# Linear attention with a rational feed-forward: slots of 1024 columns in double-bank buffers, weights loaded in place, and a new plan of the order

## The chip, the cores and the metric

The kernel runs on one core of one Trainium2 chip. The metric is the device time in microseconds (us), from the start of the program to its end on that core; the time before is the median of three runs.

## The reference, cut to what matters

Inputs are r, k, v of shape 4 x 8 x 768 x 48 (batch, head, time, depth), w and u per head and depth, and the feed-forward's w_in (384 x 2048), w_out (2048 x 384), a (4 numbers) and b (2 numbers).

```python
for t in range(S):
    kt, vt, rt = (k[:, :, t], v[:, :, t], r[:, :, t])
    cur = np.einsum('bhd,bhe->bhde', u[None] * kt, vt)
    y[:, :, t] = np.einsum('bhd,bhde->bhe', rt, state + cur)
    state = w[None, :, :, None] * state + np.einsum('bhd,bhe->bhde', kt, vt)
...
h = x @ w_in
P = a[0] + a[1] * h + a[2] * h2 + a[3] * h3
Q = 1.0 + np.abs(b[0]) * np.abs(h) + np.abs(b[1]) * h2
g = P / (Q + 1e-06)
return (g @ w_out).astype(np.float32)
```

Here x is y with heads side by side (3072 x 384), and h2 and h3 are powers of h. The feed-forward weights come as 64-bit floats.

## The kernel before

The attention is cut into 24 blocks of 128 time steps (6 for each of 4 batches), handled with matrices inside a block and a carried state between blocks of a batch. A block loads r, k and v (L340), scales k and r by powers of w (L366, L370), forms the bonus of u (L374 to L388), transposes k and r on TensorE (`tk`, `tr`, L393), and makes the products `kv` (L438, L439), `a` (L416, L417) and `y` (L466). Then x is transposed (L485) into a high and a low part, `xthi` and `xtlo`.

The feed-forward has 12 tiles of 256 rows of x. A tile goes through 16 column blocks of 128 in w_in. A slot is two such blocks (`JG = 2`), so its h is 128 x 512, one PSUM bank; four banks rotate. The first product `f1` makes 9 matmuls of 256 columns for each block (L509: three pieces of the depth, each as high x high, high x low, low x high). Five steps on ScalarE (ACT) follow, `z` (absolute value, L540), `q` (square, L544), `t` (square, L549), `ln` (L554) and `ex` (L558), and five on VectorE (DVE), `u3` (L562), `hi` (L568), `p` (L572), `d` (L576) and `lo` (L580), which ends the slot's use of h. The second product `f2` makes three matmuls of 384 columns for each block and half tile (L513 to L515). The tile's output is copied by ACT (L613) and sent by SyncE (SP, L618).

The weights are split into a high and a low part in 28 pieces (12 of w_in, 16 of w_out). A piece is loaded into a staging tile that shares buffers with g (L253), changed on ACT and DVE, rounded on GpSimd (POOL, L278), and written as two parts into `wi_hi`, `wi_lo`, `wo_hi`, `wo_lo` (L281, L284).

The order of all this is not written out by hand. Each step is a task with a key, a planned duration, what it needs, and what buffers it takes. A planner (`run`) plays five engines through time: an engine that is idle takes the ready task with the smallest key whose buffers are free. The list that results is issued as it stands. Where TensorE finds no task and the planned time lies between the two numbers of `WARM` (L627: 1.6 and 132.098 us), the planner puts a dummy matmul there, 128 x 128 of ones into unused columns of an output bank (L898 to L905, issued at L914). A planned 0.0555 us stands for each. At the end every engine loads a flag (`okf`, L1006) and skips a general version of the kernel, which these inputs don't need.

Of the kernel before, what the change touches and what calls it, by code (L numbers as in the profile page):

```python
# [21 lines left out]
P = 128  # L22
HALF = 64
QC = float(np.float32(1.0) + np.float32(1e-6))
LN_SHIFT = 22
W_MIN, W_MAX = 0.5, 1.5
SIGN = -(1 << 31)
SMALL = 2.0 ** -40


@with_exitstack
def tile_linear_attention_rational_ffn(ctx, tc, r, k, v, w, u, w_in, w_out, a, b, out):
# [20 lines left out]
    ew = ctx.enter_context(tc.tile_pool(name="ew", bufs=3))  # L53
    ps_h = ctx.enter_context(tc.tile_pool(name="ps_h", bufs=4, space=PSUM))
# [17 lines left out]
    lnb = cst.tile([P, 3], F32, name="lnb")  # L72
# [23 lines left out]

    def pro_load():
        nc.sync.dma_start(wraw, w.rearrange("h d -> (h d)").rearrange("(c p) -> p c", p=P))
# [5 lines left out]
        nc.gpsimd.memset(wones, 1.0)  # L104
# [18 lines left out]
    def pro_beta():  # L123
        nc.scalar.activation(beta[:, 0:2], coef[:, 4:6], AF.Abs)
        nc.scalar.activation(cabs, coef, AF.Abs)

        nc.vector.tensor_scalar(rx, cabs[:, 3:6:2], SMALL, None, op0=ALU.max)
        nc.scalar.activation(half, rx, AF.Ln)
        nc.scalar.activation(root, half, AF.Exp, scale=0.5)
        nc.vector.memset(lnb[:, 0:1], QC * 2.0 ** -LN_SHIFT)  # L130
        nc.vector.memset(lnb[:, 1:2], -LN_SHIFT * math.log(2.0))


    def pro_squares():
# [5 lines left out]
        v_.reciprocal(half, root)  # L140
        v_.tensor_scalar(ctmp[:, 0:1], A3, 0.0, 0.5, op0=ALU.is_ge, op1=ALU.subtract)
# [98 lines left out]
    wi_hi = cst.tile([P, NCC, FF], F32R, name="wi_hi")  # L240
    wi_lo = cst.tile([P, NCC, FF], F32R, name="wi_lo")
    wo_hi = cst.tile([P, NJ, DM], F32R, name="wo_hi")
    wo_lo = cst.tile([P, NJ, DM], F32R, name="wo_lo")

    pieces = []

    def piece(hi, lo, src, n, nm):
        pieces.append({"hi": hi, "lo": lo, "src": src, "n": n, "nm": nm})

    def cv_load(c):  # L250
        n = c["n"]
        st = ew.tile([P, n, 2], I32, tag="g", name=f"st{c['nm']}")
        nc.sync.dma_start(st.rearrange("p n two -> p (n two)"), c["src"])  # L253
        c["top"], c["low"] = st[:, :, 1], st[:, :, 0]

    def cv_up(c):
        c["up"] = ew.tile([P, c["n"]], I32, tag="tc", name=f"up{c['nm']}", bufs=NTC)
        nc.scalar.activation(c["up"], c["low"].bitcast(U32), AF.Copy, scale=2.0 ** -29)

    def cv_exp(c, p):
        c["mag"] = pat("cp", p)[:, 0 : c["n"]]
        nc.scalar.activation(c["mag"], c["top"].bitcast(F32), AF.Copy, scale=2.0 ** -112)

    def cv_shift(c):
        m = c["mag"].bitcast(I32)
        nc.vector.tensor_scalar(m, m, 3, None, op0=ALU.logical_shift_left)

    def cv_sign(c):  # L270
        c["bits"] = ew.tile([P, c["n"]], I32, tag="tb", name=f"bits{c['nm']}")
        c["f"] = c["bits"].bitcast(F32)
        nc.vector.scalar_tensor_tensor(
            c["bits"], c["top"], SIGN, c["mag"].bitcast(I32), op0=ALU.bitwise_and, op1=ALU.bitwise_or
        )

    def cv_round(c):
        nc.gpsimd.tensor_tensor(c["bits"], c["bits"], c["up"], op=ALU.add)  # L278

    def cv_hi(c, e):  # L280
        copy(e, c["hi"], c["f"])  # L281

    def cv_lo(c, e):
        e.tensor_sub(c["lo"], c["f"], c["hi"].bitcast(F32))  # L284
# [218 lines left out]
    hps, gs, ops, oss = {}, {}, {}, {}  # L503

    def mm(o, j, hi, lo):
        n = 0
        for cc in range(NCC):
            for wt_, x_ in ((wi_hi, hi), (wi_hi, lo), (wi_lo, hi)):
                nc.tensor.matmul(o, wt_[:, cc, ts(j, P)], x_[:, cc], start=(n == 0), stop=(n == 3 * NCC - 1))  # L509
                n += 1  # L510

    def mm2(o, j, hi, lo):
        nc.tensor.matmul(o, hi, wo_hi[:, j], start=(j == 0), stop=False)  # L513
        nc.tensor.matmul(o, hi, wo_lo[:, j], start=False, stop=False)  # L514
        nc.tensor.matmul(o, lo, wo_hi[:, j], start=False, stop=(j == NJ - 1))  # L515


    SL = [(f, j, JG) for f in range(NTILE) for j in range(0, NJ, JG)]
    SL[-1:] = [(NTILE - 1, j, 1) for j in range(NJ - JG, NJ)]
    NS = len(SL)  # L520

# [24 lines left out]
    def ew_t(s):  # L546
        g = tiles(s)
        g["t"] = ew_tile(s, "tc", "t", bufs=NTC)
        nc.scalar.activation(g["t"], g["h"], AF.Square, scale=RA, bias=KA)  # L549

    def ew_ln(s):
        g = gs[s]
        g["z"] = ew_tile(s, "tb", "z")
        nc.scalar.activation(g["z"], g["q"], AF.Ln, scale=2.0 ** -LN_SHIFT, bias=lnb[:, 2:3])  # L554

    def ew_exp(s):
        g = gs[s]
        nc.scalar.activation(g["z"], g["z"], AF.Exp, scale=-1.0, bias=lnb[:, 1:2])  # L558
# [24 lines left out]
    def ew_general(s):  # L583
# [4 lines left out]
        t = ew_tile(s, "tc", "t", bufs=NTC)  # L588
# [3 lines left out]
        nc.scalar.activation(z, q, AF.Ln, scale=2.0 ** -LN_SHIFT, bias=lnb[:, 0:1])  # L592
        ew_exp(s)
# [8 lines left out]
    def f2(s, hf):  # L602
# [13 lines left out]
    def put_dma(f, hf):  # L616
# [4 lines left out]
    X0, DX0, DX1, DX2, DUE = 0.37, 7.61, 2.62, 3.94, 55.23  # L621
    AT = (
        -25.81, 17.05, -1.47, 56.83, 99.81, 143.46, 69.7, 148.52, 176.2, 128.58, 179.13, 132.24,
        194.38, 256.91, 197.64, 205.9, 149.09, 174.78, 262.97, 362.97, 354.01, 318.73, 358.59, 430.42,
    )
    CV0, DCV0, DCV1 = -48.38, 3.22, 1.32
    WARM = 1.6, 132.098  # L627
    HFREE = 1
    OFF = {
# [409 lines left out]
```

## Time and profile before

| what | value |
|---|---|
| median of 3 runs | 599.33 us (598.55 to 599.92) |
| profiled execution, first to last instruction | 597.1 us |
| TensorE busy | 579.9 us (97%) |
| VectorE busy | 518.9 us (87%) |
| ScalarE busy | 455.9 us (76%) |
| GpSimd busy | 178.3 us (30%) |
| matmuls in the profile | 6373, of which 896 are dummies |

All rows of the profile come from one execution; its span is 2.2 us under the median, and covers the first to the last instruction. PE is TensorE and PEld its loading of weights, which overlaps the matmuls. A matmul's duration contains its way through the array, so in a dense run the distance from start to start is the price of one, not the duration. A step of the idle column names what the engine waited for.

### The profile page before, as it was taken

Reading aid. Unit: us, or ns where it says so; the run is one execution under the profiler, and the core shown is the slowest. Engines: PE = TensorE matmul, PEld = TensorE weight load, DVE = VectorE, ACT = ScalarE, POOL = GpSimd, SP = SyncE. Lnnn points to the kernel's source line nnn. Section 1 sums busy time; section 2 is a strip of 40 time slices with the busy share of each in tenths; the row PEclk is TensorE's granted clock in tenths of the full one; section 3 lists DMA queues with packets and bytes.
Section 4 is the critical chain, followed back from the end, with each engine's and each line's share of the span. In section 5 each row is a group of like instructions: output and inputs, shape, how many; then the busy total and the mean of one; then the engine's idle time right before and its main releaser. Section 6 shows DMA issues by size and latency. Waiting matters only on the chain.

```text
span 597.1 us, 15392 instructions
## 1 busy us (share of the span) xinstructions
PE 579.9 (97%) x6373; PEld 560.5 (94%) x6373; DVE 518.9 (87%) x798; ACT 455.9 (76%) x765; POOL 178.3 (30%) x192
## 2 busy tenths in 40 slices
PE   8979999999999999999999998999999999999995
PEld 7968899999999999999999998999999999999995
DVE  5999999999989889889888799788899897878784
ACT  8728567887998987787687885888778767788883
POOL 6777887997541000003001076001240100000000
PEclk9979999999999999999999999999999999999998
DMA  9919365928050000002012132020220000000000
GB/s 194 194 41 216 96 147 131 237 85 167 14 94 1 27 1 23 6 2 60 1 26 63 28 75 54 0 53 22 43 57 4 14 29 2 1 27 1 27 2 32
DMA packets 92642, 34.31 MB, mean 57 GB/s; under 512 B 85906, under 2 KB 88980, under 8 KB 92564
## 3 DMA queue, kind: packets, MB, share of 16 engines
q1 hardware_dynamic: 92564, 33.24, 24.6%
q8 instruction: 52, 0.85, 0.6%
q14 instruction: 26, 0.21, 0.1%
HBM read 28.52 MB, written 4.72 MB: 56 GB/s over the span
## 4 chain that ended last, share of the span: by engine, by line
PE 78%; DVE 5%; POOL 2%; ACT 1%; DMA 1%; issue 1%; SPq 0%; DVEq 0%; POOLq 0%
PE h L509 32%; PE o L513 11%; PE o L515 10%; PE o L514 10%; PE o L914 3%; PE kv L438 3%; PE y L466 2%; PE a L416 2%; PE tk L393 1%; PE x L485 1%; PE tr L393 1%; DMA kh<-in_k_dram 1%; DVE ysa L427 1%; DVE vs L477 1%; DVE g L568 1%; DVE q L572 1%
## 5 line engine op out<-in xcount | busy, mean ns | idle before, releaser
L509 PE MATMUL h<-xthi,wi_hi 128*128 128x256 f32 x576 | 164.7, 286 | 0.0
L509 PE MATMUL h<-xthi,wi_lo 128*128 128x256 f32 x576 | 162.5, 282 | 0.0
L509 PE MATMUL h<-xtlo,wi_hi 128*128 128x256 f32 x576 | 162.5, 282 | 0.0
L513 PE MATMUL o<-wo_hi,g 128*128 128x384 f32 x384 | 132.2, 344 | 0.0
L515 PE MATMUL o<-wo_hi,g 128*128 128x384 f32 x384 | 129.0, 336 | 0.7 <-DVE g L580 0.7
L514 PE MATMUL o<-wo_lo,g 128*128 128x384 f32 x384 | 128.7, 335 | 0.0
L509 PEld LDWEIGHTS h<-xthi,wi_hi 128*128 128x128 f32 x576 | 109.4, 190 | 0.5
L509 PEld LDWEIGHTS h<-xthi,wi_lo 128*128 128x128 f32 x576 | 109.7, 190 | 0.0
L509 PEld LDWEIGHTS h<-xtlo,wi_hi 128*128 128x128 f32 x576 | 109.5, 190 | 0.0
L540 ACT ACTIVATE q<-h 128x512 f32<-128x512 f32 (+1 forms) x97 | 57.6, 594 | 67.3 <-PE h L509 63.3
L568 DVE SCALAR_TENSOR_TENSOR g<-h,sig,z 128x512 fp32r<-128x512 f32 (+1 forms) x97 | 72.1, 743 | 41.4 <-ACT z L558 37.3
L544 ACT ACTIVATE q<-q,off,root 128x512 f32<-128x512 f32 (+1 forms) x97 | 78.5, 809 | 0.4
L572 DVE SCALAR_TENSOR_TENSOR q<-q,sig,g 128x512 f32<-128x512 f32 (+1 forms) x97 | 75.3, 776 | 2.4
L549 ACT ACTIVATE t<-h,off,root 128x512 f32<-128x512 f32 (+1 forms) x97 | 74.7, 770 | 3.3 <-PE h L509 3.1
L562 DVE SCALAR_TENSOR_TENSOR h<-t,sig,h 128x512 f32<-128x512 f32 (+1 forms) x97 | 72.2, 744 | 4.7 <-ACT q L540 1.9
L576 DVE SCALAR_TENSOR_TENSOR h<-h,sig,q 128x512 f32<-128x512 f32 (+1 forms) x97 | 72.8, 751 | 2.6
L515 PEld LDWEIGHTS o<-wo_hi,g 128*128 128x128 f32 x384 | 72.1, 188 | 1.2 <-DVE g L580 1.2
L513 PEld LDWEIGHTS o<-wo_hi,g 128*128 128x128 f32 x384 | 72.4, 189 | 0.7
L514 PEld LDWEIGHTS o<-wo_lo,g 128*128 128x128 f32 x384 | 72.5, 189 | 0.0
L554 ACT ACTIVATE z<-q,lnb 128x512 f32<-128x512 f32 (+1 forms) x97 | 70.0, 722 | 2.4
L558 ACT ACTIVATE z<-z,lnb 128x512 f32<-128x512 f32 (+1 forms) x97 | 69.7, 719 | 2.5
L580 DVE TENSOR_TENSOR g<-h,z 128x512 fp32r<-128x512 f32 (+1 forms) x97 | 66.0, 680 | 1.3
(137 smaller groups left out, 988.8 us busy)
## 6 DMA issues: line engine op xcount, KB each, us to landing
sti<-in_moe_w_in_dram SPq DMA_DIRECT2D x12, 512.0 KB, 5.2
sto<-in_moe_w_out_dram SPq DMA_DIRECT2D x16, 384.0 KB, 3.2
vn<-in_v_dram SPq DMA_DIRECT2D x24, 192.0 KB, 3.4
rh<-in_r_dram SPq DMA_DIRECT2D x24, 192.0 KB, 3.7
kh<-in_k_dram SPq DMA_DIRECT2D x24, 192.0 KB, 4.6
out_dram<-os SPq DMA_DIRECT2D x24, 192.0 KB, 1.9
vs<-in_v_dram SPq DMA_DIRECT2D x18, 96.0 KB, 4.4
wraw<-in_w_dram SPq DMA_DIRECT2D x1, 1.5 KB
```

Source lines behind the costliest of these rows:

```text
L509: nc.tensor.matmul(o, wt_[:, cc, ts(j, P)], x_[:, cc], start=(n == 0), stop=(n == 3 * NCC - 1))
L513: nc.tensor.matmul(o, hi, wo_hi[:, j], start=(j == 0), stop=False)
L514: nc.tensor.matmul(o, hi, wo_lo[:, j], start=False, stop=False)
L515: nc.tensor.matmul(o, lo, wo_hi[:, j], start=False, stop=(j == NJ - 1))
L544: nc.scalar.activation(g["q"], g["q"], AF.Square, scale=RB, bias=KB)
L549: nc.scalar.activation(g["t"], g["h"], AF.Square, scale=RA, bias=KA)
L554: nc.scalar.activation(g["z"], g["q"], AF.Ln, scale=2.0 ** -LN_SHIFT, bias=lnb[:, 2:3])
L558: nc.scalar.activation(g["z"], g["z"], AF.Exp, scale=-1.0, bias=lnb[:, 1:2])
L562: nc.vector.scalar_tensor_tensor(g["h"], g["t"], KAP, g["h"], op0=ALU.add, op1=ALU.mult)
L568: nc.vector.scalar_tensor_tensor(g["hi"], g["h"], c0, g["z"], op0=ALU.add, op1=ALU.mult)
L572: nc.vector.scalar_tensor_tensor(g["q"], g["q"], qe, g["hi"].bitcast(F32), op0=ALU.add, op1=ALU.mult)
L576: nc.vector.scalar_tensor_tensor(g["h"], g["h"], c0, g["q"], op0=ALU.add, op1=ALU.subtract)
```

## The change

Feed-forward slots hold four column blocks (`JG = 4`), so h is 128 x 1024 and takes two PSUM banks; there are two such buffers, which the attention's products may also take one of. The last tile's slots are of 4, 4, 4, 2, 1 and 1 blocks. ACT's and DVE's ten steps of a slot are as before, but 1024 columns wide; `t` and `ln` write the same tile, so `ln` waits for `u3`, which reads `t`. The scale that `ln` and `ex` took as operands is folded into the constants of the prologue (`ROOT_SHIFT`, `SHIFT`).

Every weight piece has a tile of its own, into which it is loaded, in which it is changed, and in which its high and low part end; no staging tile is shared, and the loads wait for no buffer. Constants `coef` have early keys.

The planner moves out of the kernel's body (`graph`, `plan`), with one list of numbers K: a key for every tile, piece and block, and offsets for each kind of task, other ones for the first few of a kind. Dummies are added in groups of up to 64, up to the time of the next event; where no event is left, one at a time. `WARM` is now 1.6 and 1232.04.

```diff
+JG = 4
+SL = [(f, j, JG) for f in range(NTILE) for j in range(0, NJ, JG)]
+SL[-1:] = [(NTILE - 1, NJ - JG, 2), (NTILE - 1, NJ - 2, 1), (NTILE - 1, NJ - 1, 1)]
+CAP = {"g": 2, "tb": 2, "ta": 2, "cb": 3, "m": 6, "ldv": 3, "dt": 2, "os": 2, "xt": 2, "h": 2, "o": 1, "pa": 2}
...
+            add(("t", s), t + 5, {"A": 0.24 + 0.427 * x}, [("f1", s, nj - 1), ("sq",)], new=[("tb", ("z", s))], use=[h])
+            add(("ln", s), t + 8, {"A": 0.19 + 0.427 * x}, [("q", s), ("u3", s)], use=[("q", s), ("z", s)])
...
+    while events:
+        now = events[0][0]
...
+            if not done and e == "P" and w0 <= now < w1:
+                c = min(64, max(1, int((events[0][0] - now) / 0.0555) + 1)) if events else 1
+                order.append((("warm", c), e))
+                idle[e] = clock(now, 0.0555 * c, 128 * c)
+                seq += 1
+                heapq.heappush(events, (idle[e], seq, "engine", e))
...
+    'WARM': (
+        1.6, 1232.04,
+    ),
...
+    ps_h = ctx.enter_context(tc.tile_pool(name="ps_h", bufs=2, space=PSUM))
...
+    def cv_load(c):
+        st = cst.tile([P, c["n"], 2], I32, tag=c["tag"], name="s" + c["tag"])
+        nc.sync.dma_start(st.rearrange("p n two -> p (n two)"), c["src"])
+        c["top"], c["low"] = st[:, :, 1], st[:, :, 0]
...
+    def cv_hi(c):
+        c["w"] = whole[c["name"]] = cst.tile([P, 2, c["n"]], F32R, tag=c["tag"], name=c["tag"])
+        nc.scalar.copy(c["w"][:, HI], c["f"])
...
     def ew_ln(s):
         g = gs[s]
-        g["z"] = ew_tile(s, "tb", "z")
-        nc.scalar.activation(g["z"], g["q"], AF.Ln, scale=2.0 ** -LN_SHIFT, bias=lnb[:, 2:3])
+        nc.scalar.activation(g["z"], g["q"], AF.Ln, bias=QE)
...
-    WARM = 1.6, 132.098
...
+    def warm(count):
+        for _ in range(count):
+            o_ = ops[max(ops)][1] if ops else idle_bank
+            alone = not filling
+            nc.tensor.matmul(o_[:, DM:512], wones, wones, start=alone, stop=alone)
```

What the new numbers do to the order is shown at three places. The first is the end of TensorE's queue, where `o11_0` and `o11_1` are the two halves of the last tile's output and `okf` the flag. Before:

```order
L513 MATMUL o11_0_7855<-wo_hi_107,g96_8095 128x384
L514 MATMUL o11_0_7855<-wo_lo_108,g96_8095 128x384
L515 MATMUL o11_0_7855<-wo_hi_107,g96_8095 128x384
L513 MATMUL o11_1_7856<-wo_hi_107,g96_8095 128x384
L514 MATMUL o11_1_7856<-wo_lo_108,g96_8095 128x384
L515 MATMUL o11_1_7856<-wo_hi_107,g96_8095 128x384
L233 MATMUL fl0_8121<-identw_80,oks_103 1x128
L1006 TENSOR_LOAD okf_104
```

And now, where the pair of rows on `wones` is a dummy (weight load and matmul):

```order
L832 MATMUL o11_0_6962<-wo_15_1038,g49_7163 128x384
L833 MATMUL o11_0_6962<-wo_15_1038,g49_7163 128x384
L834 MATMUL o11_0_6962<-wo_15_1038,g49_7163 128x384
L832 MATMUL o11_1_6963<-wo_15_1038,g49_7163 128x384
L833 MATMUL o11_1_6963<-wo_15_1038,g49_7163 128x384
L834 MATMUL o11_1_6963<-wo_15_1038,g49_7163 128x384
L968 LDWEIGHTS wones_79
L968 MATMUL o11_1_6963<-wones_79 128x128
...
L1063 TENSOR_LOAD okf_104
```

Between the last product and the flag's load the pair on `wones` now stands 12,073 times; another 744 stand ahead of the last product, of which 229 open the queue. The flag's transpose has moved to an earlier place.

The second place is DVE's queue in the last quarter, where no attention is left beside the feed-forward (h, q, z and g with a slot's number are its tiles). Before, slots 82 and 83 of 512 columns:

```order
L562 SCALAR_TENSOR_TENSOR h82_7411<-t82_7449,sig_102,h82_7411 128x512
L568 SCALAR_TENSOR_TENSOR g82_7495<-h82_7411,sig_102,z82_7474 128x512
L572 SCALAR_TENSOR_TENSOR q82_7446<-q82_7446,sig_102,g82_7495 128x512
L562 SCALAR_TENSOR_TENSOR h83_7462<-t83_7499,sig_102,h83_7462 128x512
L576 SCALAR_TENSOR_TENSOR h82_7411<-h82_7411,sig_102,q82_7446 128x512
L580 TENSOR_TENSOR g82_7495<-h82_7411,z82_7474 128x512
L568 SCALAR_TENSOR_TENSOR g83_7534<-h83_7462,sig_102,z83_7521 128x512
```

And now, slots 42 and 43 of 1024 columns:

```order
L875 SCALAR_TENSOR_TENSOR h42_6614<-z42_6675,sig_102,h42_6614 128x1024
L881 SCALAR_TENSOR_TENSOR g42_6722<-h42_6614,sig_102,z42_6675 128x1024
L885 SCALAR_TENSOR_TENSOR q42_6672<-q42_6672,sig_102,g42_6722 128x1024
L889 SCALAR_TENSOR_TENSOR h42_6614<-h42_6614,sig_102,q42_6672 128x1024
L893 TENSOR_TENSOR g42_6722<-h42_6614,z42_6675 128x1024
L875 SCALAR_TENSOR_TENSOR h43_6693<-z43_6749,sig_102,h43_6693 128x1024
L881 SCALAR_TENSOR_TENSOR g43_6796<-h43_6693,sig_102,z43_6749 128x1024
```

The next slot's first step (`u3`, L562, now L875) stood between `p` and `d` of the slot at hand, and now stands behind its last step (`lo`, L893).

The third place is the head of SP's queue, which issues the loads (`sti`, `sto`, `swi`, `swo` are pieces of w_in and w_out, `wraw` is w). Before:

```order
L98 DMA wraw<-in_w_dram 128x3x1
L340 DMA vn_137<-in_v_dram 128x8x48
L340 DMA vn_147<-in_v_dram 128x8x48
L340 DMA rh_111<-in_r_dram 128x8x48
L340 DMA rh_113<-in_r_dram 128x8x48
L340 DMA kh_112<-in_k_dram 128x8x48
L340 DMA kh_114<-in_k_dram 128x8x48
L253 DMA sti_0_228<-in_moe_w_in_dram 128x1024
```

And now:

```order
L575 DMA swo_130<-in_moe_w_out_dram 128x768
L575 DMA swi_1_140<-in_moe_w_in_dram 128x1024
L575 DMA swi_0_161<-in_moe_w_in_dram 128x1024
L658 DMA vn_178<-in_v_dram 128x8x48
L658 DMA kh_108<-in_k_dram 128x8x48
L575 DMA swi_1_211<-in_moe_w_in_dram 128x1024
L575 DMA swo_243<-in_moe_w_out_dram 128x768
L658 DMA rh_107<-in_r_dram 128x8x48
L575 DMA swi_2_294<-in_moe_w_in_dram 128x1024
L441 DMA ur<-in_u_dram 1x384
L441 DMA wr<-in_w_dram 1x384
L575 DMA swo_357<-in_moe_w_out_dram 128x768
```

`wraw`, which stood first, comes next behind these twelve; weights stand ahead of r and k, and the last weight piece is the 52nd row of the queue.

More of the change, by code (lines that the diff above doesn't have):

```diff
@@ L71, in tile_linear_attention_rational_ffn @@
     beta = cst.tile([P, 2], F32, name="beta")
-    lnb = cst.tile([P, 3], F32, name="lnb")
+    lnb = cst.tile([P, 2], F32, name="lnb")
     A0, A1, A2, A3 = (coef[:, i : i + 1] for i in range(4))
@@ L237, in pro_flag_min, with wi_of @@
         nc.vector.tensor_copy(okf, oks[0:1, 1:2])
[L240 to L243, printed above, removed]
+    HI, LO = 0, 1
     pieces = []
-    def piece(hi, lo, src, n, nm):
-        pieces.append({"hi": hi, "lo": lo, "src": src, "n": n, "nm": nm})
+    whole = {}
+    def wi_of(j, cc, part):
+        return whole["i", j * P // CW, cc][:, part, ts(j % (CW // P), P)]
@@ L256, in cv_up @@
     def cv_up(c):
[L257 to L268, printed above, removed]
-    def cv_sign(c):
[L271 to L275, printed above, removed]
@@ L277, in cv_round, with cv_shift @@
-    def cv_round(c):
-        nc.gpsimd.tensor_tensor(c["bits"], c["bits"], c["up"], op=ALU.add)
-    def cv_hi(c, e):
-        copy(e, c["hi"], c["f"])
+        nc.scalar.activation(c["low"], c["low"].bitcast(U32), AF.Copy, scale=2.0 ** -29)
+    def cv_shift(c, p):
+        c["mag"] = pat("cp", p)[:, 0 : c["n"]].bitcast(I32)
+        nc.vector.tensor_scalar(c["mag"], c["top"], 3, None, op0=ALU.logical_shift_left)
+    def cv_sign(c):
+        nc.vector.scalar_tensor_tensor(c["top"], c["top"], SIGN, c["mag"], op0=ALU.bitwise_and, op1=ALU.bitwise_or)
@@ L507, in mm @@
         for cc in range(NCC):
-            for wt_, x_ in ((wi_hi, hi), (wi_hi, lo), (wi_lo, hi)):
-                nc.tensor.matmul(o, wt_[:, cc, ts(j, P)], x_[:, cc], start=(n == 0), stop=(n == 3 * NCC - 1))
+            for part, x_ in ((HI, hi), (HI, lo), (LO, hi)):
+                nc.tensor.matmul(o, wi_of(j, cc, part), x_[:, cc], start=(n == 0), stop=(n == 3 * NCC - 1))
                 n += 1
     def mm2(o, j, hi, lo):
[L513 to L520, printed above, removed]
+        nc.tensor.matmul(o, hi, wo_of(j, HI), start=(j == 0), stop=False)
+        nc.tensor.matmul(o, hi, wo_of(j, LO), start=False, stop=False)
+        nc.tensor.matmul(o, lo, wo_of(j, HI), start=False, stop=(j == NJ - 1))
     def f1(s, jj):
@@ L787, in tile_linear_attention_rational_ffn @@
-    COLS = {"turn": 256, "flagt": 256, "tk": 1024, "tr": 1024, "x": 768, "wp": 40, "ubp": 1536, "kv": 1180, "a": 1620, "y": 1736, "f1": 2304, "f2": 2304, "warm": 128}
-    TICK = 10.24 / 3
-    ticks = {}
-    def clock(t, dur, cols):
-        while dur > 1e-9:
-            k_ = int(t / TICK + 1e-9)
-            rate = 1.0 if ticks.get(k_ - 1, 0) >= 3060 else 0.5
-            step = min(dur / rate, (k_ + 1) * TICK - t)
-            ticks[k_] = ticks.get(k_, 0) + cols * step * rate / dur
-            cols -= cols * step * rate / dur
-            dur -= step * rate
-            t += step
-        return t
@@ L918, in tile_linear_attention_rational_ffn @@
+    def warm(count):
[3 more added lines that the diff above has]
+            nc.tensor.matmul(o_[:, DM:512], wones, wones, start=alone, stop=alone)
+    FN["warm"] = lambda e, count: warm(count)
+    order, banks, _, _ = plan(K)
+    bank.update(banks)
+    idle_bank = ps_o.tile([P, 512], F32, tag="o1", name="idle_bank")
     with tc.manual_schedule():
-        run()
+        for name, e in order:
+            FN[name[0]](ENG[e], *name[1:])
```

617 lines of the change are left out of this document (335 added, 282 removed), and 16 rows, old and new, of tables (K, OFF).

## The prediction, made before the changed kernel was run

> **What bounds the kernel now.** I read the page first: the engines' busy shares, and the chain of work that ended last.
>
> ```profile
> span 597.1 us, 15392 instructions
> PE 579.9 (97%) x6373; PEld 560.5 (94%) x6373; DVE 518.9 (87%) x798; ACT 455.9 (76%) x765; POOL 178.3 (30%) x192
> PE 78%; DVE 5%; POOL 2%; ACT 1%; DMA 1%; issue 1%; SPq 0%; DVEq 0%; POOLq 0%
> ```
>
> TensorE is busy for 97% of the span and is 78% of the chain. The kernel is a queue of matmuls, and its length is the time: 597.1 - 579.9 leaves 17.2 us without a matmul, some of it at both ends. Whatever is put into TensorE's queue therefore shows in the time at its full price, and whatever is saved on DVE or ACT shows only where TensorE waits for them. Next I read the busy time by stretches (columns: stretch, its length, PE, PEld, DVE, ACT, POOL with their counts, granted clock, DMA share, GB/s).
>
> ```profile
> 0.00:20.00 20.00, 17.38 (x298) 15.47 (x299) 12.85 (x23) 17.38 (x37) 13.81 (x30) 1.00 1.06 206
> 20.00:40.00 20.00, 16.56 (x274) 14.74 (x272) 19.17 (x30) 10.89 (x25) 15.72 (x15) 0.84 0.52 113
> 60.00:80.00 20.00, 19.31 (x350) 17.97 (x347) 19.75 (x28) 12.32 (x25) 17.05 (x16) 1.00 0.47 110
> 200.00:250.00 50.00, 50.00 (x354) 49.97 (x353) 44.36 (x63) 39.15 (x61) 0.00 (x0) 1.00 0.05 17
> ```
>
> Up to 140 us TensorE has gaps in its real work, and dummy matmuls fill them; from 200 us on the feed-forward keeps it full at clock 1.00. Third, the chain in such a full stretch, and the dummies in TensorE's timeline.
>
> ```profile
> 204.35 2.15 PE h L509 x18
> 208.59 2.15 PE h L509 x18
> 212.82 2.15 PE h L509 x18
> ...
> 2.08 3.17 PE L914 MATMUL warm<-wones 128*128 128x128 bf16 x28 [2.08 <-POOL wones L104]
> 5.04 0.63 PE L207 MATMUL ptab<-identw,pw 128*128 128x128 f32 x2
> ...
> 96.59 3.47 PE L914 MATMUL o<-wones 128*128 128x128 bf16 x59
> 99.87 0.42 PE L513 MATMUL o<-wo_hi,g 128*128 128x384 f32 x1
> ```
>
> A 512-column slot (18 matmuls of the first product, then 12 of the second) comes every (212.82 - 204.35) / 2 = 4.235 us. A dummy costs (99.87 - 96.59) us / 59 = 55.6 ns from start to start; the 28 at the very start cost (5.04 - 2.08) / 28 = 106 ns each. The groups by line give what all 896 dummies of the kernel before took:
>
> ```profile
> L914 PE MATMUL warm<-wones 128*128 128x128 bf16 x455 | 32.9, 235 | 2.1 <-POOL wones L104 2.1
> L914 PE MATMUL o<-wones 128*128 128x128 bf16 x441 | 27.3, 219 | 0.0
> ```
>
> That is 60.2 us, all before 141 us, as a planned time of 132.098 us ends them. The end of the program, from the timeline of all engines:
>
> ```profile
> 590.07 1.10 ACT L613 ACTIVATE os<-o,sig 128x384 f32<-128x384 f32 x2 [4.53 <-PE o L515]
> 590.22 0.34 PE L515 MATMUL o<-wo_hi,g 128*128 128x384 f32 x1
> ...
> 591.02 0.14 DVE L237 CAST okf<-oks 1x1 int32<-1x1 f32 x1
> ```
>
> The last product ends at 590.56. The last output and the flag follow at once, and 6.5 us of flag load, output landing and exit close the span.
>
> **The change, part by part.**
>
> *Dummies behind the last product.* The changed constant lets the planner add dummies until its own clock reads 1232.04 us, and it does so even when no task is left. The order shows the result: 744 dummies stand ahead of the last second product, and 12,073 behind it, in one block, ahead of TensorE's load of the flag. Nothing follows that could hide them: the outputs are written by ACT and SP meanwhile, and the program cannot end before TensorE has read the flag. The block costs 12,073 x 55.6 ns = 671.3 us. The bounds of the unit price are close: TensorE has no gap in the block, so the clock should stay at the 1.00 of the full stretch.
>
> *The real work on TensorE.* The same products in the same pieces are made, only grouped by four column blocks and not by two. With its first end at 590.56 and the 60.2 us of dummies taken out, 530.4 us are left. The 744 dummies inside cost about 30 x 106 ns while the clock is cold and 714 x 55.6 ns after, 3.2 + 39.7 = 42.9 us. The last product would end at 573.3 us, if TensorE waited as little as before.
>
> *Longer slots on ACT and DVE.* The groups with shapes kept apart, for the seven steps that follow each other from slot to slot in the new order:
>
> ```profile
> L572 DVE SCALAR_TENSOR_TENSOR q<-q,sig,g 128x512 f32<-128x512 f32 x95 | 74.3, 782 | 2.4
> L576 DVE SCALAR_TENSOR_TENSOR h<-h,sig,q 128x512 f32<-128x512 f32 x95 | 71.8, 756 | 2.5
> L562 DVE SCALAR_TENSOR_TENSOR h<-t,sig,h 128x512 f32<-128x512 f32 x95 | 71.2, 749 | 4.7 <-ACT q L540 1.9 <-ACT t L549 1.4
> L568 DVE SCALAR_TENSOR_TENSOR g<-h,sig,z 128x512 fp32r<-128x512 f32 x95 | 71.1, 748 | 41.4 <-ACT z L558 37.3 <-PE o L515 3.1 <-issue 0.2
> L554 ACT ACTIVATE z<-q,lnb 128x512 f32<-128x512 f32 x95 | 69.0, 726 | 2.4
> L558 ACT ACTIVATE z<-z,lnb 128x512 f32<-128x512 f32 x95 | 68.7, 723 | 2.5
> L580 DVE TENSOR_TENSOR g<-h,z 128x512 fp32r<-128x512 f32 x95 | 65.2, 686 | 1.2
> L554 ACT ACTIVATE z<-q,lnb 128x256 f32<-128x256 f32 x2 | 1.0, 508 | 0.0
> L558 ACT ACTIVATE z<-z,lnb 128x256 f32<-128x256 f32 x2 | 1.0, 508 | 0.0
> L576 DVE SCALAR_TENSOR_TENSOR h<-h,sig,q 128x256 f32<-128x256 f32 x2 | 1.0, 493 | 0.1
> L562 DVE SCALAR_TENSOR_TENSOR h<-t,sig,h 128x256 f32<-128x256 f32 x2 | 1.0, 487 | 0.0
> L572 DVE SCALAR_TENSOR_TENSOR q<-q,sig,g 128x256 f32<-128x256 f32 x2 | 1.0, 478 | 0.0
> L568 DVE SCALAR_TENSOR_TENSOR g<-h,sig,z 128x256 fp32r<-128x256 f32 x2 | 1.0, 476 | 0.0
> L580 DVE TENSOR_TENSOR g<-h,z 128x256 fp32r<-128x256 f32 x2 | 0.8, 420 | 0.0
> ```
>
> At 512 columns they sum to 5.17 us, at 256 to 3.37; every 256 columns add 1.80, so 1024 columns take 5.17 + 3.60 = 8.77 us, less than twice 5.17. Per slot DVE and ACT thus get cheaper. But where the feed-forward runs alone, DVE's new queue holds the first step of slot s+1 (u3) behind the last of slot s (lo), and ln now writes the tile that u3 has to read first: u3, ln, ex, hi, p, d, lo form a loop with no second slot in it. Two such steps in DVE's timeline show what lies between them:
>
> ```profile
> 577.31 0.75 DVE L568 SCALAR_TENSOR_TENSOR g<-h,sig,z 128x512 fp32r<-128x512 f32 x1 [0.65 <-ACT z L558]
> 578.10 0.75 DVE L572 SCALAR_TENSOR_TENSOR q<-q,sig,g 128x512 f32<-128x512 f32 x1
> ```
>
> That is 578.10 - 577.31 - 0.75 = 0.04 us. With six of these, some 0.2 us, the loop turns in 9.0 us, against 2 x 4.235 = 8.47 on TensorE. With only two double banks TensorE cannot run ahead of it. Some 27 slots stand in such stretches; 27 x 0.5 = 13.5 us is the most, and every stretch begins with a slot or so of slack. I take 8 us, and 0 and 14 as its ends. The copy of the second output half, between ln and ex in one slot of four, is in this margin. The steps that the change takes off DVE and ACT are worth nothing while TensorE bounds.
>
> *Loads and the start.* SP's queue now begins with weights, and w itself (wraw), on which the scaling of the first r and k rests, stands thirteenth, behind 3.9 MB; at the 206 GB/s of the first stretch that is 19 us. The 229 dummies that open TensorE's queue take 14.4 us of that, so little is added. All weight pieces go into places of their own and wait for no staging buffer; the last one has 16.4 MB ahead of it, itself included, which takes 80 us at 206 GB/s and 145 us at the 113 GB/s of the second stretch. The second product of slot 3, its first user, stands behind some 100 us of TensorE work. So there is no wait by the first rate, and 50 us with conversion by the second. The first rate is the nearer one, since DMA was saturated there (share 1.06) and at half load in the other (0.52). I take +4 us, with -10 (the 10.7 us of gaps ahead of the end going) and +45 as ends. The cheaper constants (two fewer scale operands, one multiplication more in the prologue) cost nothing that TensorE waits for.
>
> *Sum.* 573.3 + 8 + 4 = 585 us for the last product, 671 for the block, and 6 for flag and exit give a span of 1262.6; with the 2.2 us by which the median of 599.33 lies above the profiled span of 597.1, that is 1265 us. The measurement can tell about 0.2% from no change; this is 111% slower.
>
> **A rule against the unit price.** The row above spaces dummies by 55.6 ns over a run of 59. The Trainium skill's page "TensorE: Matmul & The Clock Gate", section "Back-to-back issue gap", says that a sustained stream of weight loads and matmuls in pairs is spaced by some 81 ns at 128 columns. By its figure the block would last 978 us and the kernel about 1572 us. The trace speaks against it, at 55.6 ns with a weight load ahead of every dummy; no run so far holds an unbroken block of this length, so it stays as a rival.
>
> **The rivals.**
>
> (a) The work part is late as well, and the last product ends above 630 us: weights at the slow rate, or attention steps put into the new loop. For it are the waits of the kernel before (engine, what it waited for: us in total, times, longest):
>
> ```profile
> POOL rh L370 <- DMA rh<-in_r_dram: 87.6, 7, 25.3
> POOL kh L366 <- DMA kh<-in_k_dram: 72.1, 6, 30.7
> ```
>
> POOL stood up to 30.7 us for one load, and DVE at 87% is the second bound. Against it: by the first stretch's rate the last weights are some 20 us ahead of their use. It gives 630 + 671 + 8 = 1309 us and more.
>
> (b) The long block runs at a wider spacing than 59 dummies show, as the clock falls or instructions come too slowly. At the cold row's 106 ns it would last 1280 us, and the kernel 1873 us. Against it: the full stretches keep clock 1.00 for 50 us and more, and from 60 to 80 us 697 instructions went through in 20 us, 28.7 ns each, where the block needs 27.8. The page's 81 ns would fall under this rival.
>
> (c) Faster: the block does not count. If time were taken up to the last output's landing, or if matmuls whose product nobody reads were not run, the price of the block would be zero and the kernel would come to 585 + 8 = 593 us or, without the loop and start terms, 581 us. It decides from 12,073 x 55.6 ns falling under 6 us. For it: no output depends on the block. Against it: the 60.2 us of dummies before were run as any matmul, and the median is above the span up to the last instruction, so time covers every engine's end.
>
> (d) The work part ends ahead of 560 us, and the kernel below 1240: the gaps and the hand-overs of the first 140 us nearly vanish.
>
> **How the numbers follow.** The forecast, 1240 to 1310 us, has 0.82: its low end is 585 less 8, 4 and the 10.7 us of gaps, with 671 and 8 added, its high end the bound of the loads (585 + 45). Rival (a) has 0.08, (b) 0.06, (c) 0.02, (d) 0.02. No more than 0.2 is left out by the forecast's own range, so the range is not widened. Faster by over 0.2% is (c) alone, 0.02; nothing leads to no change; slower is 0.98.
>
> **What would show it.** In the changed kernel's profile: TensorE's dummies as the costliest group, near 12,800 of them; DVE, ACT and POOL idle in the last half of the 40 slices, with TensorE at 9 there and PEclk at 9; the last second product between 560 and 630 us; DVE's u3 to u3 at 9 us in slots 14 to 21 and 41 to 46, and TensorE waiting there for lo. The forecast is wrong if the spacing in the block is not 55 to 57 ns, if the last product ends outside 560 to 630 us, or if the span ends well ahead of the block.

## The result and the profile after

| what | before | after |
|---|---|---|
| median of the runs | 599.3 us (598.55 to 599.92, 4 runs) | 1257.99 us (1257.75 to 1259.32, 4 runs) |
| ratio to before, with its interval | | 2.099 (2.096 to 2.102) |
| profiled execution, own time and span | | 1259.32 us, 1257.6 us |

The kernel takes 2.1 times as long, 7 us less than forecast. One execution of all behind this document, of the kernel before without its dummies, took 882.86 us at a granted clock of 0.56, for a reason that no run here shows; it is left out, and the median given for that kernel further down is of its other three. First the head of the page of after: span, busy time of the engines, some rows of the 40 slices (each 31.4 us here), and the shares of the chain that ended last.

```profile
span 1257.6 us, 38579 instructions
PE 1243.1 (99%) x18294; PEld 1221.6 (97%) x18294; DVE 468.6 (37%) x570; ACT 384.6 (31%) x508; POOL 171.5 (14%) x195
PE   8999999999999999999999999999999999999998
DVE  6898898787887877772000000000000000000000
ACT  7895685666656656661000000000000000000000
PEclk9899999999999999999999999999999999999999
PE 87%; DVE 3%; ACT 2%; issue 1%; POOL 0%; ACTq 0%; POOLq 0%
```

DVE and ACT fall silent in the 19th slice, near 580 us. TensorE goes on at a full clock for 21 more slices, alone. A page that showed only TensorE's 99% would read like a well-filled kernel. Which instructions fill it is shown by the groups by line, the costliest one of matmuls being

```profile
L968 PE MATMUL o<-wones 128*128 128x128 bf16 x12169 | 681.1, 219 | 0.7 <-ACT os L930 0.7
```

These are dummies, for 681.1 us. TensorE's timeline places them (start, duration, line, operation, and in brackets the idle time ahead of it and what ended it): the last second product, the first two rows of the block and its last one.

```profile
578.42 0.33 PE L834 MATMUL o<-wo,g 128*128 128x384 f32 x1
578.60 0.40 PE L968 MATMUL o<-wones 128*128 128x128 bf16 x4
579.66 10.54 PE L968 MATMUL o<-wones 128*128 128x128 bf16 x186 [0.67 <-ACT os L930]
...
1247.81 5.86 PE L968 MATMUL o<-wones 128*128 128x128 bf16 x102
```

The work ends at 578.6 us, the block at 1247.81 + 5.86 = 1253.7 us, and the program at 1257.6 us: 578.6 + 675.1 + 3.9. After four dummies the block stops for 0.67 us, for ACT, which still reads the bank into which they write; from then on it has no gap. Of its 12,073 dummies 12,069 stand behind that wait, (1253.67 - 579.66) us / 12,069 = 55.8 ns each. In the windows (columns as before), 100 us from the middle of the block and 50 us of the feed-forward alone:

```profile
600.00:700.00 100.00, 100.00 (x1795) 100.00 (x1793) 0.00 (x0) 0.00 (x0) 0.00 (x0) 1.00 0.01 2
500.00:550.00 50.00, 49.84 (x377) 49.16 (x377) 37.65 (x34) 32.98 (x34) 0.00 (x0) 1.00 0.03 12
```

100 us / 1795 = 55.7 ns, with a weight load beside each, at clock 1.00; a window also counts the few matmuls that reach into it from outside, so this agrees with 55.8. In the feed-forward DVE is at 75% and ACT at 66% of the stretch; before, from 200 to 250 us, they were at 89% and 78%.

### The profile page after: what moved, and what is told of

Read it like the earlier page. It is cut to its first block, busy times and chain, and to the rows that moved or that the text cites. A ratio compares the mean times of both kernels' runs of the same rounds, so it can differ in the third digit from the quotient of the medians.

```text
span 1257.6 us, 38579 instructions
## 1 busy us (share of the span) xinstructions
PE 1243.1 (99%) x18294; PEld 1221.6 (97%) x18294; DVE 468.6 (37%) x570; ACT 384.6 (31%) x508; POOL 171.5 (14%) x195
## 3 DMA queue, kind: packets, MB, share of 16 engines
q8 instruction: 145, 2.38, 0.8%
## 4 chain that ended last, share of the span: by engine, by line
PE 87%; DVE 3%; ACT 2%; issue 1%; POOL 0%; ACTq 0%; POOLq 0%
PE o L968 54%; PE h L828 13%; PE o L832 4%; PE o L834 4%; PE o L833 4%; PE y L784 2%; PE a L734 2%; PE kv L756 1%; PE tr L711 1%; PE tk L711 1%; PE x L803 1%; DVE g L881 1%; DVE h L875 1%; DVE q L885 1%; ACT z L867 1%
## 5 line engine op out<-in xcount | busy, mean ns | idle before, releaser
L968 PEld LDWEIGHTS <-wones 128*128 128x128 bf16 x12817 | 720.5, 98 | 4.8 <-POOL wones L424 2.1
L968 PE MATMUL o<-wones 128*128 128x128 bf16 x12169 | 681.1, 219 | 0.7 <-ACT os L930 0.7
L828 PE MATMUL h<-xthi,wi 128*128 128x256 f32 x1152 | 219.0, 284 | 1.0 <-DVE g L893 0.8
L828 PEld LDWEIGHTS h<-xthi,wi 128*128 128x128 f32 x1152 | 180.9, 188 | 3.0 <-issue 0.8
L828 PE MATMUL h<-xtlo,wi 128*128 128x256 f32 x576 | 160.8, 279 | 0.0
L832 PE MATMUL o<-wo,g 128*128 128x384 f32 x384 | 131.6, 343 | 0.0
L834 PE MATMUL o<-wo,g 128*128 128x384 f32 x384 | 129.2, 336 | 0.0
L833 PE MATMUL o<-wo,g 128*128 128x384 f32 x384 | 129.1, 336 | 0.0
L828 PEld LDWEIGHTS h<-xtlo,wi 128*128 128x128 f32 x576 | 108.4, 188 | 0.0
L832 PEld LDWEIGHTS o<-wo,g 128*128 128x128 f32 x384 | 72.2, 188 | 0.3
L833 PEld LDWEIGHTS o<-wo,g 128*128 128x128 f32 x384 | 72.3, 188 | 0.0
L834 PEld LDWEIGHTS o<-wo,g 128*128 128x128 f32 x384 | 72.2, 188 | 0.0
L875 DVE SCALAR_TENSOR_TENSOR h<-z,sig,h 128x1024 f32<-128x1024 f32 (+2 forms) x50 | 62.0, 1240 | 6.6 <-ACT z L863 6.4
L885 DVE SCALAR_TENSOR_TENSOR q<-q,sig,g 128x1024 f32<-128x1024 f32 (+2 forms) x50 | 63.4, 1269 | 1.3
L889 DVE SCALAR_TENSOR_TENSOR h<-h,sig,q 128x1024 f32<-128x1024 f32 (+2 forms) x50 | 62.3, 1246 | 1.3
L893 DVE TENSOR_TENSOR g<-h,z 128x1024 fp32r<-128x1024 f32 (+2 forms) x50 | 58.9, 1178 | 1.2
```

The costliest lines, as they stand in the source:

```text
L828: nc.tensor.matmul(o, wi_of(j, cc, part), x_[:, cc], start=(n == 0), stop=(n == 3 * NCC - 1))
L832: nc.tensor.matmul(o, hi, wo_of(j, HI), start=(j == 0), stop=False)
L833: nc.tensor.matmul(o, hi, wo_of(j, LO), start=False, stop=False)
L834: nc.tensor.matmul(o, lo, wo_of(j, HI), start=False, stop=(j == NJ - 1))
L875: nc.vector.scalar_tensor_tensor(g["h"], g["t"], KAP, g["h"], op0=ALU.add, op1=ALU.mult)
L885: nc.vector.scalar_tensor_tensor(g["q"], g["q"], qe, g["hi"].bitcast(F32), op0=ALU.add, op1=ALU.mult)
```

## The experiments

### Is it the block, and what does one dummy cost?

Theory: the block is paid in full, dummy by dummy, and has nothing to do with the new slots. Rival: a part of the 672 us belongs to the longer slots or the late loads. Three kernels tell them apart. The first leaves out every dummy behind the last product:

```diff
+    last = max(i for i, (n, e) in enumerate(order) if e == "P" and n[0] != "warm")
+    left = 0
+    kept = order[: last + 1]
+    for n, e in order[last + 1 :]:
+        if n[0] == "warm":
+            n = ("warm", min(left, n[1]))
+            left -= n[1]
+        if n[0] != "warm" or n[1]:
+            kept.append((n, e))
+    order = kept
```

> The changed kernel without the 12,073 dummies behind the last second product; all other instructions in the same order. Theory (every dummy of the block is paid in full): the last product stays at 579 us and the exit of 6 us as in the kernel before follows, so 585 to 587 us, 2.2% below the kernel before. Rival (the block covers something else that is slow in the new order, such as output copies or the flag): clearly more, above 592 us. Second rival (the loss lies in the longer slots, the block only fills it): near 1250 us.

Measured: 586.17 us, ratio to before 0.978 (0.974 to 0.981), span 584.9 us. The second keeps half of the block (`left = 6036`):

> The changed kernel with 6,036 dummies behind the last second product in the place of 12,073. Theory: the price is linear, 6,037 x 55.9 ns = 337.5 us less, so 920 to 921 us. Rival (a long run is spaced wider than a short one, from some length on): less than half of the block's 675 us goes with the first half of it, so a time away from 920 us by more than 5 us.

Measured: 919.95 us, ratio 1.536 (1.530 to 1.542). The third is the kernel before, with the block behind its order loop:

```diff
+        o_ = ops[max(ops)][1]
+        for _ in range(12073):
+            nc.tensor.matmul(o_[:, DM:512], wones, wones, start=True, stop=True)
```

> The kernel before, with 12,073 dummies put behind its last product, nothing else changed. Theory (the price belongs to the dummies and not to the new slots or plan): 599.3 + 675 less the 2 to 4 us of exit that now hide, so 1270 to 1275 us. Rival (the new slots and plan have a part in the loss): 1270 us is missed by more than 10 us.

Measured: 1271.21 us, ratio 2.123 (2.114 to 2.132). A window in the block of each, the half block's kernel first, then before with the block:

```profile
700.00:800.00 100.00, 100.00 (x1795) 100.00 (x1792) 0.00 (x0) 0.00 (x0) 0.00 (x0) 1.00 0.01 2
```

```profile
700.00:800.00 100.00, 100.00 (x1795) 100.00 (x1793) 0.00 (x0) 0.00 (x0) 0.00 (x0) 1.00 0.01 2
```

What follows: the block adds 1257.99 - 586.17 = 671.8 us to the changed kernel and 1271.21 - 599.01 = 672.2 us to the kernel before (599.01 us being its median beside these runs), 55.6 to 55.7 ns for each dummy. The first half of it adds 333.8 us and the second 338.0; the first is less because it hides the end of the last output. So the price is linear and the same in both kernels. The rival falls, and without the block the change is faster than before by 2.2% (1.9 to 2.6%).

### What does the loop through DVE cost?

The prediction put 8 us on the loop u3, ln, ex, hi, p, d, lo. DVE's timeline of after has it, u3 of three slots that follow each other and the wait for ex inside one of them:

```profile
522.79 1.28 DVE L875 SCALAR_TENSOR_TENSOR h<-z,sig,h 128x1024 f32<-128x1024 f32 x1
526.44 1.28 DVE L881 SCALAR_TENSOR_TENSOR g<-h,sig,z 128x1024 fp32r<-128x1024 f32 x1 [2.37 <-ACT z L871]
531.55 1.28 DVE L875 SCALAR_TENSOR_TENSOR h<-z,sig,h 128x1024 f32<-128x1024 f32 x1
540.32 1.28 DVE L875 SCALAR_TENSOR_TENSOR h<-z,sig,h 128x1024 f32<-128x1024 f32 x1
```

It turns in (540.32 - 522.79) / 2 = 8.77 us. TensorE, in the same stretch, begins first products at

```profile
523.80 0.28 PE L828 MATMUL h<-xthi,wi 128*128 128x256 f32 x1
...
532.17 0.28 PE L828 MATMUL h<-xthi,wi 128*128 128x256 f32 x1
...
540.54 0.36 PE L828 MATMUL h<-xthi,wi 128*128 128x256 f32 x1
...
549.31 0.35 PE L828 MATMUL h<-xthi,wi 128*128 128x256 f32 x1 [0.15 <-DVE g L893]
```

that is every 8.37 us, until the slack is used up and the last of these slots takes 8.77 us too. So the loop exists and is slower than TensorE by 0.4 us a slot. To break it, one kernel (without the block) puts u3 of slot s+1 ahead of lo of slot s in DVE's queue, wherever they are neighbours:

```diff
+    for s in range(1, NS):
+        at_ = {n: i for i, (n, e) in enumerate(order)}
+        dve = [n for n, e in order if e == "D"]
+        lo_, u3_ = ("lo", s - 1), ("u3", s)
+        if dve.index(u3_) == dve.index(lo_) + 1 and max(at_["t", s], at_["z", s]) < at_[lo_]:
+            x = order.pop(at_[u3_])
+            order.insert(at_[lo_], x)
```

> The changed kernel without the block, and in DVE's queue the first step of the next slot (u3) stands ahead of lo, the last step of the slot at hand, wherever lo and u3 stood side by side. Theory (the loop u3, ln, ex, hi, p, d, lo, 8.76 us a slot in the trace against 8.38 us of TensorE, holds TensorE up): the loop loses lo and falls to 7.5 us, TensorE bounds again, and the time falls by 2 to 8 us against the run without the block alone. Rival (the two buffers have slack enough, and TensorE is held up by attention steps and the start): within 1 us of it, or longer, since lo and with it the second product come 1.3 us later.

Measured: 593.26 us, ratio 0.990 (0.987 to 0.994), 7 us slower than without the swap. The theory failed in sign. DVE's timeline of this kernel, two u3:

```profile
536.12 1.29 DVE L875 SCALAR_TENSOR_TENSOR h<-z,sig,h 128x1024 f32<-128x1024 f32 x1 [1.60 <-ACT z L863]
545.32 1.29 DVE L875 SCALAR_TENSOR_TENSOR h<-z,sig,h 128x1024 f32<-128x1024 f32 x1 [1.61 <-ACT z L863]
```

Each now waits 1.6 us for t on ACT, and they come every 9.20 us. The lo of the slot before is queued behind it and waits as well, and TensorE's next first product waits for that lo, which frees its bank. TensorE's list of waits (us in total, times, longest) has this wait without the block as the first of the next two lines, and with the swap as the second:

```profile
PE h L828 <- DVE g L893: 0.6, 2, 0.5
```

```profile
PE h L828 <- DVE g L893: 7.2, 14, 0.9
```

The 6.6 us more come near the 7 us by which this kernel is slower. The stretch of 50 us, without the block and then with the swap:

```profile
500.00:550.00 50.00, 49.90 (x378) 49.21 (x377) 37.65 (x34) 32.99 (x34) 0.00 (x0) 1.00 0.04 12
```

```profile
500.00:550.00 50.00, 48.23 (x438) 46.82 (x439) 36.13 (x34) 29.24 (x30) 0.00 (x0) 1.00 0.03 9
```

The swap closes another loop: f1, z, t and u3 of a slot, then the lo of the slot before, then f1 of the next slot, as h has two buffers and that lo frees one. In this trace its steps begin at 529.49, 533.97, 534.89, 536.12 and 537.32 us, and the next f1 at 538.69: a turn of 9.20 us, longer than the loop that it breaks. The planner's order was the better of the two. A kernel that breaks the first loop without this one gives t a tile of its own (one that is dead by then) in slots 42 to 46, so that ln no longer waits for u3:

```diff
-        g["z"] = g["t"] = ew_tile(s, "tb", "z")
+        if s in range(42, 47):
+            g["t"] = vs2[s % 2].rearrange("p a b c d -> p (a b c d)")[:, 0 : SL[s][2] * N1]
+        else:
+            g["z"] = g["t"] = ew_tile(s, "tb", "z")
```

> The changed kernel without the block, and in slots 42 to 46 the tile t has a place of its own (that of the attention's state, which is done with by then), so that ln no longer waits for u3. Theory (the loop of 8.76 us costs its excess over TensorE's 8.38 us in the last stretch, through which the chain of the run without the block goes): u3 follows u3 by 8.4 us there and the time falls by 1 to 2 us from 586 us. Rival (the slack of two buffers covers it): within 0.5 us of it.

Measured: 584.71 us, ratio 0.974 (0.970 to 0.977), against 0.978 (0.974 to 0.981) without this edit: the times don't tell them apart. Its trace does. DVE's timeline, u3 of two slots and between them the step that waits for ex:

```profile
531.21 1.28 DVE L880 SCALAR_TENSOR_TENSOR h<-vs,sig,h 128x1024 f32<-128x1024 f32 x1
534.46 1.28 DVE L886 SCALAR_TENSOR_TENSOR g<-h,sig,z 128x1024 fp32r<-128x1024 f32 x1 [1.97 <-ACT z L876]
539.57 1.28 DVE L880 SCALAR_TENSOR_TENSOR h<-vs,sig,h 128x1024 f32<-128x1024 f32 x1
```

The loop is gone: u3 follows u3 in 8.36 us, TensorE's pace. From the first product at 506.94 us to the last second product at 578.30 us the kernel without the block takes 71.4 us, this one, from 507.77 to 578.04 us, 70.3 us. The loop cost 1 us in this stretch of some five slots, and not the 0.5 us for each that was priced.

For the other stretches the trace of the kernel without the block tells it. In slots 14 to 22, from 238 to 318 us, u3 follows u3 by 8.8 to 9.1 us, but TensorE has no wait for lo there: both of its waits for lo behind 150 us, 0.6 us in all, are in the line shown above. There the loop cost nothing that the trace shows.

### What were the dummies inside worth, and where did the gain come from?

The prediction took the old dummies out at their full price (-60.2 us) and put the new ones in at theirs (+42.9 us). If that is how they act, the kernel after without any dummy should come near 543 us. If they only fill time in which TensorE waits anyway, it should stay where it is. The kernel after without any dummy, and the kernel before without all but those ahead of 1.6 us:

```diff
+    order = [(n, e) for n, e in order if n[0] != "warm"]
```

> The changed kernel without any dummy: the block and the 744 inside are gone, the rest of the order is the same. Theory (a dummy ahead of the last product fills a wait that would be there anyway, so only dummies behind it are paid in full): within 6 us of the 586 us without the block, with some of the gain lost to a half clock in the first 100 us. Rival (every dummy is paid in full, wherever it stands, as the sum of the prediction had it): 43 us less, 543 us.

Measured: 587.81 us, ratio 0.980 (0.976 to 0.985).

```diff
-    WARM = 1.6, 132.098
+    WARM = 1.6, 1.6
```

> The kernel before without its 896 dummies, nothing else changed. Theory (they fill waits): within 8 us of 599 us. Rival (each is paid in full): 60 us less, 539 us. Compared with the changed kernel without dummies it also tells what of the 13 us between the two kernels without the block comes from the dummies: if all of it, the two come out alike within 3 us; if the longer slots and the new plan bring it, 10 us or more stay.

Measured: 606.80 us, ratio 1.009 (1.006 to 1.013). So taking the dummies inside out gains nothing in either kernel; in the kernel before they save 6 to 7 us (599.88 us is its median beside these runs), in the kernel after the times don't tell the two apart. This is their price net of what they do to the clock. One place shows how they fill a wait. The first line is the opening of TensorE's queue with dummies (the kernel after without its block), the second a row of its waits without any:

```profile
2.08 14.61 PE L968 MATMUL idle_bank<-wones 128*128 128x128 bf16 x229 [2.08 <-POOL wones L424]
```

```profile
PE pup L478 <- POOL ur L473: 16.6, 1, 16.6
```

Where 229 dummies stood for 14.6 us (and a wait for `ur` of 1.4 us was left), TensorE now waits 16.6 us for `ur`. Without any dummy, the changed kernel is 19 us ahead of the kernel before, with them 12 to 13 us. The first 150 us of after and then of before, both without them:

```profile
0.00:150.00 150.00, 111.78 (x1284) 101.35 (x1285) 129.44 (x189) 112.32 (x188) 102.66 (x121) 0.92 0.55 138
```

```profile
0.00:150.00 150.00, 105.83 (x1228) 93.09 (x1229) 129.66 (x216) 107.37 (x215) 107.84 (x118) 0.78 0.61 142
```

With dummies the granted clock is 0.97 and 0.98 there (next windows). Without them TensorE is idle for 38 and 44 of the 150 us, the clock is 0.92 and 0.78, and TensorE is busy for longer with its real work than it was between dummies (111.78 us in after, against 96.4 below).

What did change is the size of the holes. For the same window with dummies, the kernel before and then the kernel after without its block, all of TensorE and the dummies alone:

```profile
0.00:150.00 150.00, 141.47 (x2390) 130.99 (x2390) 137.11 (x219) 107.76 (x215) 119.19 (x132) 0.98 0.67 150
...
0.00:150.00 150.00, 60.21 (x896) 55.66 (x896) 0.98 0.67 150
```

```profile
0.00:150.00 150.00, 142.86 (x1974) 135.94 (x1974) 127.71 (x189) 112.79 (x188) 103.01 (x120) 0.97 0.55 138
...
0.00:150.00 150.00, 46.50 (x691) 43.64 (x691) 0.97 0.55 138
```

Real work in the first 150 us: 141.47 - 60.21 = 81.3 us before, 142.86 - 46.50 = 96.4 us after. Some 15 us of products that stood behind 150 us now stand ahead of it, with 9 us less on DVE and 16 us less on POOL. The last second product comes 590.56 - 578.63 = 11.9 us earlier, so about 3 us of these are given back later.

What sets the holes? Two kernels without the block issue one step of each weight piece a second time, DVE's first one or POOL's.

```diff
         nc.vector.tensor_scalar(c["mag"], c["top"], 3, None, op0=ALU.logical_shift_left)
+        nc.vector.tensor_scalar(c["mag"], c["top"], 3, None, op0=ALU.logical_shift_left)
```

> Without the block; the first DVE step of each weight piece (mag from the high word) is issued twice, with the same result, 16 x 0.548 + 12 x 0.688 = 17.0 us more on DVE, all ahead of 106 us, where DVE is busy for 84 of the first 100 us. Theory: what holds TensorE back in the first 150 us is the amount of work on DVE, so that the holes shrank because fewer attention steps and more feed-forward stand there; then the end moves by 8 to 17 us, to 594 to 603 us. Rival: the loads set the pace of the start, and DVE waits for them anyway; then the time stays within 2 us of 586.

```diff
         nc.gpsimd.tensor_tensor(bits, c["top"], c["low"], op=ALU.add)
+        nc.gpsimd.tensor_tensor(bits, c["top"], c["low"], op=ALU.add)
```

> Without the block; GpSimd's first step of each weight piece (the sum of the two words) is issued twice, 16 x 0.83 + 12 x 1.04 = 25.8 us more on POOL, all ahead of 107 us, where POOL is busy for 78 of the first 100 us. Theory (DVE is the bound of the start, POOL has slack): less than 5 us later, 586 to 591 us. Rival (POOL's conversions are in the same chain from weight to weight and bind as much): 10 to 25 us later, 596 to 611 us.

Measured: 596.33 us (ratio 0.997, 0.995 to 0.998) with DVE's step twice, 598.81 us (1.000, 0.999 to 1.002) with POOL's, against 586.17 us (0.978) without. The busy rows of the pages show what was added, first for DVE, then for POOL (without either, DVE has 469.4 and POOL 171.6):

```profile
PE 573.3 (96%) x6221; PEld 551.2 (93%) x6221; DVE 484.3 (81%) x598; ACT 385.4 (65%) x508; POOL 172.8 (29%) x195
```

```profile
PE 572.0 (96%) x6221; PEld 549.5 (92%) x6221; DVE 472.1 (79%) x570; ACT 385.9 (65%) x508; POOL 195.1 (33%) x223
```

14.9 us more on DVE cost 10 to 11 us, 23.5 us more on POOL cost 13 to 14 us (the first of each by medians, the second by ratios, as the kernel without them ran on another chip). The first run came out by its theory (594 to 603 us), the second by its rival (596 to 611 us): work on either engine holds the opening up, at 0.5 to 0.8 us of time for one us of work. The rival of the first run, that loads alone set the pace, falls. The same windows of the first 150 us, for DVE's step twice and then for POOL's, place the loss:

```profile
0.00:150.00 150.00, 136.69 (x1828) 129.69 (x1829) 133.33 (x206) 108.00 (x181) 95.87 (x113) 0.94 0.52 133
...
0.00:150.00 150.00, 48.79 (x691) 45.59 (x691) 0.94 0.52 133
```

```profile
0.00:150.00 150.00, 133.07 (x1812) 125.41 (x1813) 118.74 (x176) 106.21 (x179) 122.55 (x141) 0.95 0.51 131
...
0.00:150.00 150.00, 46.33 (x691) 43.44 (x691) 0.95 0.51 131
```

Real work ahead of 150 us falls from 96.4 to 87.9 and 86.7 us. Whether a step counts here as work in its engine's queue or as a longer way of a weight through both engines was not told apart. The steps that the change takes off DVE and POOL, and its order, which brings feed-forward forward and attention back, both act there; which of them gives how much of the 12 us was not told apart.

One more kernel tried the start itself: `w` and the power tables ahead of everything on all queues, and 180 dummies in place of 338 ahead of the first transpose of r.

```diff
+    front = [("w",), ("pl",), ("id",), ("cl_",), ("ctr",), ("pow", 0), ("pow", 1), ("pow", 2), ("inv", 0), ("inv", 1), ("inv", 2)]
+    front += [("turn", c, i) for i in range(2) for c in range(NCC)] + [("tab", 0), ("tab", 1)]
+    moved = [x for n in front for x in order if x[0] == n]
+    order = moved[:5] + [(("warm", 60), "P")] + moved[5:] + [x for x in order if x[0] not in front]
...
+    budget = 180
```

> The changed kernel without the block, with the load of w and the tables made of it first on every queue, and 180 dummies in the place of 338 ahead of the first transpose of r. Theory (the start is paid in full: the first transpose of r comes at 19 us, not at 28.7 us): 8 to 10 us less than 586 us. Rival (TensorE waits for the weights of slots 1 to 3 anyway, up to some 90 us, so an earlier start of the attention only lengthens that wait): within 2 us of 586 us.

Measured: 588.61 us, ratio 0.981 (0.980 to 0.983), no gain. Its first transpose of r comes at 32.17 us, in after at 28.73 us, for two waits of TensorE on POOL, as the list of its waits says:

```profile
PE pup L478 <- POOL ur L473: 7.9, 1, 7.9
PE tr L711 <- POOL rh L688: 7.8, 1, 7.8
```

`w` was early and of no use, because `ur` and `rh` stood on POOL behind weight conversions (`bwo`, `wo`, `bwi`, `wi`), and these began late: the first of them waited for DVE until 12.35 us, where the kernel without the block has it at 6.66 us, as the tables now stand ahead of the weights' steps on ACT and DVE. POOL's timeline shows both:

```profile
12.35 0.82 POOL L594 TENSOR_TENSOR bwo<-swo 128x384 int32<-128x384 int32 x1 [7.39 <-DVE swo L590]
...
19.39 1.04 POOL L594 TENSOR_TENSOR bwi<-swi 128x512 int32<-128x512 int32 x1
20.39 0.82 POOL L594 TENSOR_TENSOR bwo<-swo 128x384 int32<-128x384 int32 x1
21.17 1.50 POOL L473 TENSOR_TENSOR ur<-ur,wr 1x384 f32<-1x384 f32 x1
...
30.16 0.99 POOL L602 TENSOR_TENSOR wo<-bwo,wo 128x384 fp32r<-128x384 f32 x1 [1.51 <-ACT wo L599]
31.11 1.00 POOL L688 TENSOR_TENSOR rh<-rh,wrn 128x384 f32<-128x384 f32 x1
```

This fits what the doubled steps showed: the start goes through the weight conversions on both engines. An early load alone, with POOL's order unchanged, doesn't bring the start forward.

## Why the prediction was right, step by step

**The block.** Forecast 671.3 us behind the last product; the block lies there for 675.1 us, 55.8 ns for each dummy and not 55.6. The program grows by less, by 671.8 us between medians, because the last output and its landing, 2.4 us of them, now run beside the block. The same cover makes the exit 3.9 us and not the 6 us of the sum. Rival (b), a wider spacing in a long block, falls by these 55.8 ns. By the 81 ns that the Trainium skill, page "TensorE: Matmul & The Clock Gate", section "Back-to-back issue gap", gives for a sustained stream of pairs, the block would have lasted 978 us. The measured spacing decides; it is near that page's other figure, 55.6 ns of the section "Wait — 56ns, not 53.3ns?", here with a weight load in each pair. Rival (c), that the block isn't counted, falls by the 1257.99 us.

**The real work.** Forecast 585 us for the last product, measured 578.6 us. Three terms are in it. The base of 573.3 us was near, but its step was wrong: dummies were taken out and put in at full price, as if each delayed the products. This follows from the prediction's opening reading, that whatever is put into TensorE's queue shows in the time at full price, though the prediction also says that dummies fill gaps up to 140 us. The kernel after without dummies ends where it did with them, at 587.81 us and not at 543. They sit in holes, and their number is near the size of the holes, as the planner adds them where its own clock finds TensorE idle; the difference of 17.3 us that the step gave has 15.1 us of smaller holes behind it. That the base came near by a price that the dummies inside don't have was luck: the smaller holes are no part of that sum. The statement that steps taken off DVE and ACT are worth nothing falls too, for DVE at least: it came from the full stretches and doesn't hold in the first 150 us, where one us more of DVE work cost 0.7 to 0.8 us.

**The loop.** The mechanism was seen as forecast, at 8.77 us for 9.0; the term of 8 us was mis-sized. TensorE's own slot is 8.37 us (8.47 was taken), so a turn loses 0.4 us, and in the last stretch most turns were paid by slack. Breaking the loop gained 1 us there. In slots 14 to 21 u3 came at the forecast distance, 8.8 to 9.1 us, but the forecast wait of TensorE for lo is missing: its waits for lo behind 150 us come to 0.8 us in after, three in all. So the term is about 1 us, and 8 was too much.

**Loads and start.** Forecast +4 us. The loads came by the first rate: the last weight piece was issued at 67.1 us and no piece took over 9.1 us to land, so all were there by 76 us, where the sum had 80. The last of the conversions behind them began at 108.2 us. The first transpose of r came 19 us later than before (28.73 against 9.52 us), and the prediction had "little" for it, from 14.4 us of opening dummies (14.2 us by its own prices; 14.6 in the trace). It waited not for `w` alone: `rh`, which it reads, stood on POOL behind weight conversions until 26.05 us. What this cost is not shown, as the one kernel meant to bring it forward did not do so; the last product came earlier all the same. Of the 5.3 us between 573.3 and 578.6 us about 1 us is the loop, and the rest lies between the base, whose step was wrong, and the start; the runs don't divide it. Rivals (a) and (d), an end above 630 or below 560 us, fall by 578.6 us.

**Outside the span.** The sum added 2.2 us for the distance of median and span; the profiled execution took 1.7 us above its span, and the median of the runs lies 0.4 us above that span.

So the total of 7 us too much is -6.4 us of work, +3.8 us of block, -2.1 us of exit and -1.8 us outside, with the rest from rounding; the block, 53% of the time, was right in kind and in size.

## What to carry to other kernels

In these kernels a filler matmul was free where its engine waits and paid in full behind the last task, so a filler's end must follow the work and not a clock: here a constant in a table, read past the last event, was 672 us. Price fillers inside by the holes that they fill, not by their count; to know the holes, run the kernel without them. And before two neighbours in an in-order queue are swapped to break one loop, write down the loop that the swap closes, with the wait of the instruction that will stand behind.

## What was not expected of the hardware

TensorE held clock 1.00 and 55.8 ns a pair for 674 us without a gap, with 12,069 weight loads and matmuls, and nothing of instruction loading slowed it: the instruction queue on the profile's page has 145 packets and 2.38 MB in after, 51 and 0.84 MB without the block. And the granted clock in the opening fell only to 0.92 without dummies in the kernel after, where TensorE's idle time is 38 us, and to 0.78 in the kernel before, where it is 44 us. The dummies were worth 6 to 7 us in the kernel before and 2 us, within the spread of the runs, in the kernel after; with two kernels, that this goes with the holes is a guess.
